# Long convolution with an FFT beside a gated MLP, forward and backward: transforms that share weights run jointly over 256 columns, spectra products are written in place, and the slots are ordered anew

## The chip, the cores and the metric

One core of a Trainium2 chip runs the whole program. The metric is the device time of one execution in microseconds (us), lower is better. Before the change it is 1892.35 us, the median of three runs (1892.13 to 1892.92).

The engines that matter are TensorE (PE; PEld stands for its weight loads), VectorE (DVE), ScalarE (ACT) and the DMA queue of SyncE (SP).

## The reference, cut to what matters

All tensors are bfloat16. S = 2048, D = 1024, F = 3584.

```
xn  = layernorm(x)
out = x + xn * (fftconv(kshift * v, ssm_k) + kshift * v * ssm_D) + W_down(relu(xn W_gate) * (xn W_up))
kshift[t] = sum over 4 taps of k[t - i] * shift_k[i]
```

The kernel returns `out` and the gradients of x, k, v, shift_k, ssm_k, ssm_D, W_gate, W_up and W_down for a given `grad_out`. The convolution is causal and is done per channel with a transform of length 4096 over the zero-padded sequence. Three spectra are needed in each channel: H of the filter, K of kv = kshift * v, and G of g = grad_out * xn. Three products are transformed back:

- Y = H * K gives y, which scales xn in the output;
- GKV = conj(H) * G gives the gradient of kv, and from it those of k, v and the taps;
- GH = conj(K) * G gives the gradient of the filter.

## The kernel before, in words

Class `LnMlp` does the layer norm and the MLP: `hidden` (gate, up and the gradient of h, with loops over 14 half blocks), then `grad_down` and `grad_in` (weight gradients), then `out_phase` and `grad_x`. Its matmuls are 128 x 128 weights by 512 columns. They are cut into steps of eight matmuls; after each step the generator yields 1730 (ns).

Class `ABranch` does the convolution in eight groups of 128 channels. Each transform of length 4096 is two matmul stages with a rearrangement between them:

- `fwd1` and `fwd1_filter`: stage one with the weights `R`, in 32 x 64 tiles of the array, 8 matmuls of 512 columns a slot. ScalarE (`act`, L76) takes the result from PSUM to a tile `B`.
- `flip`: VectorE transposes blocks of 32 x 32 (L298), in two halves.
- `fwd2`: stage two with the weights `FW`, in 64 x 32 tiles, 64 matmuls of 128 columns a slot. H, G and K have each two slots.
- `turn` and `cmul`: VectorE prepares and multiplies two spectra (all through the helper `tt`, L80). `cmul` works in two halves; a half is five pieces: two wide products t, twice a product u with its sum, and last a pair of sums that write the result.
- `inv_a`: first stage back, with the weights `IA` in 32 x 64 tiles, again 64 matmuls of 128 columns in each of two slots. ScalarE takes it to a tile `C`, and `flip` follows.
- `inv_b` (weights `RB`) and `inv_b_chan`: last stage back, to time order and to channel order.

`halo`, `tap_sums`, `tap_diagonals` and `taps` make the shifted k and the tap gradients.

`slots` is the order of one group, written out by hand: a list of pairs (TensorE work, VectorE work). The main loop takes MLP steps and counts down a budget; when it is used up it inserts the next slot. A slot costs 1900 of the budget in `hidden`, so that most slots are one step apart and some are two. In the dense phase, `grad_down` and `grad_in`, a slot with TensorE work costs 1760 and one without 1250, so that two slots can follow each other with no step between. Inside this stretch each engine runs its instructions in program order.

The convolution's PSUM pool has two tiles of two banks (`ps`, tag aps), and the MLP four of one bank. Five tiles of a pool `frm` hold spectra and, earlier, the rows of x for the layer norm; three of a pool `big` hold B, C and the flipped data in turn.

MLP work on VectorE in `hidden`: after an up step L972 and L974 (the gate's mask and the product h), after a gradient step L1067 (which follows the evacuation L1066 on ScalarE), after a gate step none. In the dense phase there is none.

Of the kernel before, what the change touches and what calls it, by code (L numbers as in the profile page):

```python
# [48 lines left out]
class ABranch:  # L49
# [48 lines left out]
    def open(self):  # L98
        R = "right"
        self.con = self.pool("a_con", 1, side=R)  # L100
        self.lng = self.pool("a_lng", 1, side=R)
        self.ld = self.pool("a_ld", 1, side=R)
        self.ts = self.pool("a_ts", 3, side=R)
        self.big = self.pool("a_big", 3, side=R)
        self.frm = self.pool("a_frm", 5, side=R)
        self.tmp = self.pool("a_tmp", 2, side=R)
        self.xp = self.pool("a_xt", 1, side=R)
        self.sm = self.pool("a_sm", 2, side=R)
        self.ps = self.pool("a_ps", 2, space=bass.MemoryType.PSUM)

# [180 lines left out]
    def flip(self, st, key, src):  # L291

        dst = st[key] = self.big.tile([P, NB1, P], BF16, name="flp", tag="big")
        df = dst[:].rearrange("p k c -> p (k c)").bitcast(F32).rearrange("p (k cp) -> p cp k", cp=64)
        sf = src.rearrange("p cp r i -> p (cp r i)").bitcast(F32).rearrange("p (cp r) -> p cp r", cp=64)
        for c0 in range(0, 64, 32):
            self.pri.late()
            self.pri.pin(self.nc.vector.transpose(out=df[:, c0:c0 + 32, :], in_=sf[:, c0:c0 + 32, :]))  # L298
            yield
# [36 lines left out]
    def fwd2(self, st, key, flp):  # L336
        F, Bf = self.form(key), st[flp]
        st[key] = F
# [14 lines left out]
    def form(self, name):  # L353
        return self.frm.tile([P, 8, 2, 2, P], BF16, name=name, tag="frm")

    def turn(self, st, name, b, sign):

        F, plus, minus = st[name], ALU.add, ALU.subtract
        for i in range(2):
            x = F[:, :, b, i]  # L360
            self.tt(x, x, F[:, :, 1 - b, 1 - i], plus if (i == 0) == (sign < 0) else minus)

    def cmul(self, st, m, n, conj, name):

        M, N = st[m], st[n]
        Q = st[name] = self.form(name)
        e, f = (1, 0) if conj else (0, 1)
        for hf in range(2):
            g = slice(4 * hf, 4 * hf + 4)
            M0 = M[:, g, 0:1].to_broadcast([P, 4, 2, 2, P])  # L370
            t = []
            for i in range(2):
                t.append(self.tmp.tile([P, 4, 2, 2, P], BF16, name="t%d" % i, tag="tmp"))
                self.tt(t[i][:], M0, N[:, g, :, ::-1] if i else N[:, g], ALU.mult)
                yield
            for i in range(2):
                u = self.sm.tile([P, 4, 2, P], BF16, name="u", bufs=1)
                self.tt(u[:], M[:, g, 1], N[:, g, e, ::-1] if i else N[:, g, e], ALU.mult)
                self.tt(t[i][:, :, f], t[i][:, :, f], u[:], ALU.add)
                yield  # L380
            for i in range(2):
                self.tt(Q[:, g, :, i], t[i][:, :, :, 0], t[i][:, :, :, 1], ALU.add if conj == (i == 0) else ALU.subtract)
            yield

    def inv_a(self, st, key, q_name):
        C = st[key] = self.big.tile([P, 64, 4, 8, 2], BF16, name="C", tag="big")
        Q = st[q_name]
# [17 lines left out]
    def inv_b(self, st, key, flp):  # L405
        dst, Cf = self.ttile(key), st[flp]
# [12 lines left out]
    def inv_b_chan(self, st, flp):  # L419
        dst, Cf = self.ttile("ghn"), st[flp]  # L420
        st["ghn"] = dst
        dv = dst[:, 0:16, :].rearrange("p r c -> p (r c)").rearrange("p (n1 n2) -> p n1 n2", n2=NB1)
        for n0 in range(0, NB1, 16):
# [4 lines left out]
            yield  # L428
# [48 lines left out]
    def steps(self):  # L477
# [19 lines left out]
        self.pri.strict = True  # L497
        self.begin(nx)
        for gi in range(self.NG):
            st, nx = nx, None  # L500
# [7 lines left out]
    def begin(self, st):  # L508
        st["ksh"] = self.lng.tile([P, 16, P], BF16, name="ksh")
        st["tk"] = self.taps(st, st["ksh"], st["kp"], [(3, 0), (2, 1), (1, 2), (0, 3)])  # L510
        st["f1h"] = self.fwd1_filter(st)

    MERGED = 3

    def slots(self, st, gi):
        last = gi + 1 == self.NG
        kp, gt = st["kp"], st["gt"]

        def next_filter():
            if not last:  # L520
                st["nx"] = self.load_filter(gi + 1)

        def next_g():
            if not last:
                self.load_g(st["nx"])

        def next_xn():
            if not last:
                self.load_xn(st["nx"])

        def next_v():
            if not last:
                self.load_v(st["nx"])

        def next_k():
            if not last:
                self.load_k(st["nx"])
                self.load_taps(st["nx"])

        def next_gate():  # L540
            if not last:
                self.gate_grad(st["nx"])

        def start_kvt():
            kvt = st["kvt"] = self.ttile("kvt")
            self.tt(kvt[:, 0:16, :], st["ksh"][:], st["vt"][:], ALU.mult)

        def start_gv():
            gv = self.ttile("gv")
            self.tt(gv[:, 0:16, :], st["gkv"][:, 0:16, :], st["ksh"][:], ALU.mult)  # L550
            st["gv"] = gv

        def start_gks():
            gks = st["gks"] = self.ttile("gks")
            self.tt(gks[:, 0:16, :], st["gkv"][:, 0:16, :], st["vt"][:], ALU.mult)

        def store_y():
            self.store_time(self.y_d, st["cg"], st["yt"])

        if gi and gi <= self.MERGED:  # L560
            self.begin(st)
        tk, f1h = st["tk"], st["f1h"]
        f1g = self.fwd1(st, "Bg", gt)
        if gi <= self.MERGED:
            yield f1h, None if gi else tk
            yield f1h, tk
            yield None, self.both(lambda: self.add_D(st), tk)
            yield None, tk
            yield None, tk
        flH = self.flip(st, "fH", st["Bh"][:].rearrange("p b x cp n i -> p (b x cp) n i"))  # L570
        f2H = self.fwd2(st, "H", "fH")
        if gi == 0:
            yield None, flH
            yield None, flH
            yield None, tk
            yield None, tk
            yield f2H, None
            yield None, next_filter
            yield f2H, lambda: self.gate_grad(st)
            yield f1g, None  # L580
            yield None, None
            yield f1g, None
            flG = self.flip(st, "fG", st["Bg"][:].rearrange("p b cp u r i -> p (b cp) (u r) i"))
            yield None, next_g
            yield None, flG
            yield None, flG
        else:
            yield f1g, flH
            yield None, self.both(next_filter, flH)
            yield f1g, tk  # L590
            yield next_g, tk
            yield f2H, tk if gi <= self.MERGED else None
            flG = self.flip(st, "fG", st["Bg"][:].rearrange("p b cp u r i -> p (b cp) (u r) i"))
            yield None, flG
            yield f2H, flG
        yield None, start_kvt
        f2G = self.fwd2(st, "G", "fG")
        yield f2G, None
        yield None, next_xn
        yield f2G, None  # L600
        f1k = self.fwd1(st, "Bk", st["kvt"])
        yield f1k, lambda: self.turn(st, "G", 0, -1)
        q = self.cmul(st, "H", "G", True, "GKV")
        yield None, q
        yield f1k, q
        yield None, q
        yield None, q
        flK = self.flip(st, "fK", st["Bk"][:].rearrange("p b cp u r i -> p (b cp) (u r) i"))
        yield None, flK
        yield None, flK  # L610
        yield None, q
        yield None, q
        f2K = self.fwd2(st, "K", "fK")
        yield f2K, q
        yield None, q
        yield f2K, q
        iaG = self.inv_a(st, "Cg", "GKV")
        yield iaG, q
        yield None, lambda: self.turn(st, "H", 1, 1)
        qy = self.cmul(st, "H", "K", False, "Y")  # L620
        yield next_gate, qy
        yield iaG, qy
        yield None, qy
        yield None, qy
        yield None, qy
        flg = self.flip(st, "fCg", st["Cg"][:].rearrange("p cp q m i -> p cp (q m) i"))
        yield None, flg
        yield None, flg
        iaY = self.inv_a(st, "Cy", "Y")
        yield iaY, qy  # L630
        yield None, qy
        yield self.inv_b(st, "gkv", "fCg"), qy
        yield None, qy
        yield None, start_gv
        yield None, qy
        self.store_time(self.out_gv, st["cg"], st["gv"])
        yield None, start_gks
        qh = self.cmul(st, "K", "G", True, "GH")
        yield iaY, qh
        yield None, self.both(next_v, qh)  # L640
        yield lambda: self.halo(st), qh
        yield None, qh
        yield lambda: self.tap_sums(st), qh
        yield None, lambda: self.tap_diagonals(st)
# [883 lines left out]
```

## Time and profile before

| | busy, us | share of the span |
|---|---|---|
| TensorE matmul | 1861.8 | 99% |
| TensorE weight load (overlaps) | 870.3 | 46% |
| VectorE | 1047.2 | 55% |
| ScalarE | 616.0 | 33% |

The profiled span is 1889.3 us. The first convolution slot starts at 112.8 us and the last at about 1171; `hidden` ends at about 653, and `out_phase` begins at about 1305. VectorE is busy 64.9% of the first 100 us, 70 to 85% of each 100 us from 100 to 1100, and little later. A convolution line of the profile is that of the helper which records it (L72 for every matmul, L76 for every evacuation, L80 for every elementwise operation), so groups are told apart by the names of their tiles. Matmuls of different tiles of the array overlap: the busy time of such a group is the union, and the mean of one says nothing of the rate.

### The profile page before, as it was taken

To read this page: it belongs to the slowest core of one execution; us is meant where nothing else is said; L and a number is where in the kernel's file an instruction comes from. 1 tells how busy PE (TensorE), PEld (TensorE's weight loads), DVE (VectorE), ACT (ScalarE), POOL (GpSimd) and SP (SyncE) were. 2 spreads that over 40 slices of the span, in tenths; PEclk is the share of its full clock that TensorE was granted. 3 is DMA by queue.
4 is the path that set the end of the run, shared out by engine and by line. 5 is a ranking of instruction groups with operands and counts; after the bars stand their busy time and mean duration, and the time that the engine had idled before them with its cause. 6 is when DMAs were issued, how large, how long until landed. Compare 5 with 4: busy or idle time off the path is not lost.

```text
span 1889.3 us, 36593 instructions
## 1 busy us (share of the span) xinstructions
PE 1861.8 (99%) x15526; PEld 870.3 (46%) x15768; DVE 1047.2 (55%) x1528; ACT 616.0 (33%) x858; POOL 14.9 (1%) x37
## 2 busy tenths in 40 slices
PE   9999999999999999999999999999999999999999
PEld 4444444444444444444444444444444544444444
DVE  6667978987987886867767585000222232222222
ACT  5655345436435445454354543111000000000000
POOL 1000000000000000000000000000000000000000
PEclk9999999999999999999999999999999999999999
DMA  9897679878578657475564535923999955545553
GB/s 254 247 224 186 156 191 200 202 184 183 143 184 199 196 165 179 118 176 183 145 159 118 157 94 161 323 96 101 251 245 241 245 125 123 123 122 123 123 122 73
DMA packets 694052, 323.19 MB, mean 171 GB/s; under 512 B 524408, under 2 KB 663424, under 8 KB 693888
## 3 DMA queue, kind: packets, MB, share of 16 engines
q1 hardware_dynamic: 683392, 299.99, 64.2%
q10 hardware_dynamic: 9216, 16.65, 3.1%
q0 software_dynamic: 1280, 4.20, 0.6%
q8 instruction: 123, 2.02, 0.4%
q14 instruction: 41, 0.34, 0.1%
HBM read 143.79 MB, written 95.44 MB: 127 GB/s over the span
## 4 chain that ended last, share of the span: by engine, by line
PE 97%; issue 1%; DVE 1%; DMA 0%; ACT 0%; DVEq 0%
PE ps_x L1385 20%; PE ps_w L1158 20%; PE ps_h L868 10%; PE ps_u L868 10%; PE ps_g L868 10%; PE ps_o L1316 10%; PE ps_d L1158 9%; PE ps L72 6%; PE ps_d L1171 1%; PE ps_w L1171 1%; PE ps_r L1346 0%; DMA ugs<-ug_d 0%; PE pst_x L900 0%; DMA ln_x<-in_A_q_dram 0%; ACT ln_j L796 0%
## 5 line engine op out<-in xcount | busy, mean ns | idle before, releaser
L1158 PE MATMUL ps_w<-ugs,xn_nat 128*128 128x512 bf16 x1670 | 375.4, 379 | 5.6 <-issue 3.8
L868 PEld LDWEIGHTS <-xnT 128*128 128x128 bf16 x1792 | 171.0, 98 | 206.5 <-issue 4.1
L1158 PEld LDWEIGHTS <-xn_nat 128*128 128x128 bf16 x1728 | 164.6, 98 | 198.1 <-issue 4.9
L868 PE MATMUL ps_u<-wu,xnT 128*128 128x512 bf16 x866 | 202.8, 379 | 2.3 <-issue 1.1
L868 PE MATMUL ps_h<-wdT,goT 128*128 128x512 bf16 x862 | 201.7, 379 | 3.3 <-issue 2.2
L1403 ACT ACTIVATE w<-xn,m 128x512 f32<-128x512 bf16 x32 | 24.3, 807 | 553.0 <-issue 317.2
L868 PE MATMUL ps_g<-wg,xnT 128*128 128x512 bf16 x868 | 200.8, 379 | 2.8 <-issue 1.0
L1385 PE MATMUL ps_x<-wuT,guT 128*128 128x512 bf16 x878 | 197.5, 379 | 1.0
L1385 PE MATMUL ps_x<-wgT,ggT 128*128 128x512 bf16 x878 | 197.3, 379 | 0.9
L1316 PE MATMUL ps_o<-wd,hT 128*128 128x512 bf16 (+1 forms) x879 | 186.7, 372 | 0.9
L1158 PE MATMUL ps_d<-g_nat,hs 128*128 128x512 bf16 x735 | 168.0, 379 | 3.8 <-issue 2.9
L1308 DVE TENSOR_TENSOR ya<-ya,xe 128x1024 bf16<-128x1024 bf16 x16 | 11.1, 693 | 253.4 <-DMA xe<-xn_d 253.4
L1385 PEld LDWEIGHTS <-guT 128*128 128x128 bf16 x896 | 87.7, 98 | 105.7
L1385 PEld LDWEIGHTS <-ggT 128*128 128x128 bf16 x896 | 87.7, 98 | 105.5
L1316 PEld LDWEIGHTS <-hT 128*128 128x128 bf16 x896 | 87.7, 98 | 99.9
L868 PEld LDWEIGHTS <-goT 128*128 128x128 bf16 x896 | 84.8, 98 | 102.5 <-issue 4.2
L1387 DVE CUSTOM_DVE_ANT_0 gx<-ps_x,gy 128x512 f32<-128x512 f32 x32 | 22.1, 691 | 186.7 <-PE ps_x L1385 184.6
L1066 ACT CAST gh<-ps_h 128x512 bf16<-128x512 f32 x112 | 65.5, 587 | 173.2 <-PE ps_h L868 160.7
L1262 ACT CAST wi<-ps_w 128x512 bf16<-128x512 f32 x108 | 63.7, 590 | 172.4 <-PE ps_w L1158 163.5
L972 DVE SCALAR_TENSOR_TENSOR ru<-ru,ps_u 128x512 bf16<-128x512 bf16 x112 | 76.4, 682 | 68.4 <-PE ps_u L868 33.4
L76 ACT CAST C<-ps 128x1024 bf16<-128x1024 f32 x96 | 92.5, 1015 | 64.8 <-PE ps L72 63.4
L1158 PEld LDWEIGHTS <-hs 128*128 128x128 bf16 x768 | 71.9, 98 | 86.7 <-issue 4.0
(163 smaller groups left out, 1701.0 us busy)
## 6 DMA issues: line engine op xcount, KB each, us to landing
ug_d<-ru SPq DMA_DIRECT2D x112, 256.0 KB
ugs<-ug_d SPq DMA_DIRECT2D x112, 256.0 KB
wg<-in_B_W_gate_dram SPq DMA_DIRECT2D x56, 256.0 KB
wu<-in_B_W_up_dram SPq DMA_DIRECT2D x56, 256.0 KB
h_d<-ht SPq DMA_DIRECT2D x112, 128.0 KB
hs<-h_d SPq DMA_DIRECT2D x56, 256.0 KB
out_dram<-wi SPq DMA_DIRECT2D x56, 256.0 KB
gt<-in_grad_out_dram SPq DMA_DIRECT2D x32, 256.0 KB
```

The lines of the kernel that those rows point to most:

```text
L72: self.pri.pin(self.nc.tensor.matmul(out, lhsT=lhsT, rhs=rhs, start=start, stop=stop))
L76: self.pri.pin(self.nc.scalar.copy(out=out, in_=in_))
L868: self.pri.pin(self.nc.tensor.matmul(ps[:], lhsT=xT[:, kt * P:(kt + 1) * P], rhs=w(kt), start=(kt == 0), stop=(kt == self.DT - 1)), always ...
L972: self.pri.pin(nc.vector.scalar_tensor_tensor(out=ru[s][:, 1, :], in0=ru[s][:, 0, :], scalar=0.0, in1=ps[:], op0=ALU.is_gt, op1=ALU.mult))
L1066: self.pri.pin(nc.scalar.copy(out=gh[:], in_=ps[:]))
L1158: self.pri.pin(self.nc.tensor.matmul(ps[:], lhsT=lhsT(st), rhs=rhs(st), start=(st == 0), stop=(st == self.ST - 1)))
L1171: self.pri.pin(self.nc.tensor.matmul(ps[i][:], lhsT=lhsT(i, st), rhs=rhs(i, st), start=(st == 0), stop=(st == self.ST - 1)))
L1262: self.pri.pin(nc.scalar.copy(out=wo[0][:, d, :], in_=ps[:]))
L1316: nc.tensor.matmul(ps, lhsT=hT[:, kt, :], rhs=self.wd[:, kt, oc], start=(kt == 0), stop=(kt == self.FT - 1))
L1385: nc.tensor.matmul(ps, lhsT=T[:, kt, :], rhs=W[:, kt, oc], start=(i == 0), stop=(i == n - 1))
L1387: V.tensor_tensor_reduce(out=gx[:, oc], in0=ps, in1=gy[:, oc], scale=1.0, scalar=0.0, op0=ALU.add, op1=ALU.add, accum_out=m[:, ob:ob + 1])
L1403: nc.scalar.activation(out=w[:, oc], in_=xn[:, oc], func=ACT.Identity, scale=m[:, 7:8], bias=m[:, 6:7])
```

## The change: what it does and what it is for

G and K are transformed by the same weights FW, and GH and Y by the same weights IA. The changed kernel keeps G and K interleaved in one tile, so that one matmul can take the columns of both: 256 instead of 128, with one weight load. `fwd2_pair` does this for G and K, `inv_a_pair` for GH and Y, each in four slots of 32 matmuls, where there were four of 64. `fwd2` stays for H and `inv_a` for GKV. In the pair functions each slot writes to both PSUM tiles at once; in `inv_a_pair` the evacuation splits into four of 512 elements for each slot.

The five spectrum tiles of `frm` become one tile, the arena: two halves for flipped data, two for G and K, one for H. GH is written over G and Y over K, half by half. The rows of the layer norm move to a pool of their own, which is given back before the arena takes its place.

Since K and G have to be ready together, stage one of a group's kv moves to the end of the group before. The order of the slots is written anew; `inv_b_chan` becomes one slot. In the new order flK (flip of K) is followed directly by the first slot of `fwd2_pair`, the last piece of the last product by the third slot of `inv_a_pair`, and `start_kvt` directly by `fwd1` of kvt. In the diff tk and tg are the taps' pieces, q a product's pieces, fl* the flips.

```diff
+    def fwd2_pair(self):
+        for j in range(4):
+            ps = [self.ps.tile([P, 2, 2, 2, 2, 64], F32, name="ps2", tag="aps") for _ in range(2)]
+            for m in range(2):
+                for ri in range(2):
+                    for q in range(4):
+                        for e in range(2):
+                            rows, l = slice(64 * e, 64 * e + 64), 8 * q + 2 * j + m
+                            self.mm(ps[e][32 * q:32 * q + 32, m, :, :, ri, :], self.FW[rows, l, ri, :],
+                                    self.flp[rows, :, l, :].rearrange("p k (b c) -> p b k c", b=2))
+            for e in range(2):
+                self.act(self.GK[:, 2 * j + e].rearrange("p b k i (m c) -> p (b k i) m c", m=2),
+                         ps[e][:].rearrange("p m b k i c -> p (b k i) m c"))
+            yield
...
+    def inv_a_pair(self, Cs):
...
+                            self.mm(ps[q // 2][64 * e:64 * e + 64, q % 2, m].rearrange("p k b c -> p b k c"),
+                                    self.IA[rows, x, ri].rearrange("p a n -> p (a n)"),
+                                    self.GK[rows, 2 * j + e, :, :, ri, 64 * m:64 * m + 64],
+                                    start=ri == 0, stop=ri == 1)
+            for h in range(2):
+                for k in range(2):
+                    self.act(Cs[k][:, :, 2 * h:2 * h + 2, 2 * j:2 * j + 2, :],
+                             ps[h][:, :, :, k].rearrange("p q m b (cp i) -> p (b cp) q m i", i=2))
+            yield
...
     def slots(self, st, gi):
...
+        f2 = self.fwd2_pair()
+        yield f2, None
+        yield None, none if last else lambda: self.load_g(nx)
+        yield f2, None
+        yield None, none if last else lambda: self.load_xn(nx)
+        yield f2, None
+        yield None, lambda: self.turn(G, 0, -1, slice(0, 4))
...
+        yield f2, q
...
+        yield None, flg
+        yield None, flg
+        yield None, q
+        ibg = self.inv_b(st, "gkv", 0)
+        yield ibg, q
...
+        ia = self.inv_a_pair((Ch, Cy))
...
+        yield ia, tg
+        yield None, tg
...
+        yield ia, tg
...
+        q = self.cmul(H, K, False, K, 1)
+        yield None, q
+        yield None, q
+        yield None, q
+        yield None, q
+        yield None, q
...
+            yield ia, tk
             yield None, tk
+            yield ia, tk
             yield None, tk
+            yield f2H, tk
+        fly = self.flip_C(Cy, 0)
+        yield None, fly
+        yield f2H, fly
+        flh = self.flip_C(Ch, 1)
+        yield None, flh
+        yield self.inv_b(st, "yt", 0), flh
+        yield None, tk
+        self.store_time(self.y_d, st["cg"], st["yt"])
+        yield self.inv_b_chan(st, 1), tk
...
+        yield None, lambda: self.start_kvt(nx)
+        f1k = self.fwd1(nx, "Bk", nx["kvt"])
+        flG = self.flip_B(nx, "Bg", 0)
+        yield f1k, flG
+        yield None, flG
+        yield f1k, lambda: self.store_gh(st)
+        yield None, None
+        flK = self.flip_B(nx, "Bk", 1)
         yield None, flK
         yield None, flK
```

## The prediction, made before the changed kernel ran

> **What bounds the kernel now.** I read the page's busy times and its chain first, then the groups by shape on TensorE, then the timelines of weight loads, VectorE and TensorE around single slots.
>
> ```profile
> span 1889.3 us, 36593 instructions
> ...
> PE 1861.8 (99%) x15526; PEld 870.3 (46%) x15768; DVE 1047.2 (55%) x1528; ACT 616.0 (33%) x858; POOL 14.9 (1%) x37
> ...
> PE 97%; issue 1%; DVE 1%; DMA 0%; ACT 0%; DVEq 0%
> ```
>
> TensorE is busy 99% of the span and is 97% of the chain, so the time is its work plus whatever it is made to wait. In the stretch that holds the convolution (113 to 1172 us) VectorE is the next engine:
>
> ```profile
> 300.00:400.00 100.00, 98.41 (x1116) 46.47 (x1116) 85.44 (x117) 47.10 (x64) 0.41 (x1) 1.00 0.90 204
> ```
>
> The columns after the length are PE, PEld, DVE, ACT busy. VectorE has 15% to spare here and 29% at 1000 to 1100 us, so it keeps pace only where a slot of TensorE comes late enough after the VectorE work that it needs.
>
> The convolution's matmuls (all of L72) come in slots between steps of eight MLP matmuls. The two shapes that the change touches, the second for GKV and GH as well:
>
> ```profile
> L72 PE MATMUL ps<-flp,FW 64*32 64x128 bf16 x3072 | 36.4, 221 | 0.0
> ...
> L72 PE MATMUL ps<-Y,IA 32*64 32x128 bf16 x1024 | 12.4, 224 | 0.0
> ```
>
> Tiles overlap, so what a slot costs is read from the weight loads:
>
> ```profile
> 131.74 3.33 PEld L868 LDWEIGHTS <-xnT 128*128 128x128 bf16 x16
> 135.50 0.60 PEld L72 LDWEIGHTS <-FW 64*32 64x32 bf16 x64 [0.42 <-issue]
> 136.18 1.41 PEld L868 LDWEIGHTS <-goT 128*128 128x128 bf16 x8
> 138.01 0.12 PEld L72 LDWEIGHTS <-R 32*64 32x64 bf16 x8 [0.42 <-DVE gt L80]
> 138.36 3.14 PEld L868 LDWEIGHTS <-goT 128*128 128x128 bf16 x16 [0.23 <-issue]
> ```
>
> An undisturbed MLP matmul takes 0.216 us (3.45 us for 16 in the chain). From the end of the first line (135.07) to that of the third (137.59) are 2.52 us with eight of them: the FW slot cost 0.79. The R slot after it: 141.50 - 137.59 - 16 x 0.216 = 0.46. Done for all 192 slots, the medians are FW 0.79 (48 slots), IA 0.80 (48), R 0.46 (48), RB 0.66 (16), tap sums 1.11 (8), 0.47 for 16 matmuls of inv_b_chan; together 128.8 us, with no slot over 0.4 above its median. TensorE is hardly ever kept waiting.
>
> **What the Trainium skill says.** "TensorEngine Tiling (Array Packing)", Tiling Modes: 64x32 and 32x64 tiling give eight independent tiles, and a change of tiling mode drains TensorE. "TensorE: Matmul & The Clock Gate", Back-to-back issue gap: N/2.4 + 2.5 ns warm, 215.8 ns for 512 columns; the trace has 216. With both, R (one round of eight tiles at 213 ns by columns; 8 matmuls of 512 columns) leaves 0.25 us fixed, RB (16 x 512, two rounds) 0.24, the tap sums (64 x 128, 16 rounds of four tiles at 53 ns) 0.26: the trace agrees, eight abreast and about 0.25 us per switch. "PSUM — Partial Sum Buffer", Specifications: eight banks of 512 fp32 per partition; the convolution's two tiles of two banks, beside the MLP's four, leave no spare; no run here shows the limit itself. "TensorE: Matmul & The Clock Gate", Step-by-step: only weight loads move forward, matmuls stay in program order; so one slot that waits for VectorE holds back all MLP matmuls behind it.
>
> **The change part by part.**
>
> *Wider matmuls.* fwd2 of G and K and inv_a of Y and GH: per group 4 + 4 slots of 64 matmuls over 128 columns become 4 + 4 of 32 over 256. That is 2048 matmuls and weight loads fewer, 64 slots repriced. FW's 0.79 - 0.25 = 0.54 for eight rounds is 67 ns a round, 14 above the 53 by columns. Four rounds at 107 ns give 0.68 with no excess, 0.73 with 14 ns each. I take 0.70: 32 x 0.09 + 32 x 0.10 = 6 us gained (4 to 7; nothing if all the excess stays, 0.79).
>
> *Costs at nothing.* The in-place products, the arena and the split turn keep VectorE's work (the split adds some 0.1 us a group, beside matmuls). inv_b_chan in one slot: 2 x 0.47. ScalarE gets 16 evacuations of 512 for 8 of 1024 per group in inv_a_pair: 16 x 0.59 - 8 x 1.02 = 1.3 us a group more on an engine that is half idle. Loads lead their use by at least 14 slots of 1.7 us, about 24; the first loads took some 12 (hn issued at 100.4, used at 112.8).
>
> *The new order.* It shortens the lead of some VectorE results over the slot that needs them from two or more slots to one. How close the old order is:
>
> ```profile
> 552.69 0.68 DVE L972 SCALAR_TENSOR_TENSOR ru<-ru,ps_u 128x512 bf16<-128x512 bf16 x1
> 553.40 0.42 DVE L974 TENSOR_TENSOR ht<-ru 128x512 bf16<-128x512 bf16 x1
> 553.75 1.28 DVE L80 TENSOR_TENSOR GH<-t 128x1024 bf16<-128x1024 bf16 x2
> ```
>
> ```profile
> 549.93 3.62 PE L868 MATMUL ps_u<-wu,xnT 128*128 128x512 bf16 x15
> 553.39 1.89 PE L868 MATMUL ps_h<-wdT,goT 128*128 128x512 bf16 x8
> 555.21 0.76 PE L72 MATMUL ps<-GH,IA 32*64 32x128 bf16 x64
> ```
>
> GH was put after the first of these two up steps, two steps (3.45 us) ahead of its slot, and was ready at 555.03, 0.18 before it: VectorE first had to finish the up step's work. After the change the third inv_a_pair slot stands one step (1.73) after its last product (the last q, then `yield ia, tk`), with steps u, u, product, h, slot in group 0. With the same backlog it comes 1.73 - 0.18 = 1.5 us late. I added the durations (up 0.68 + 0.39, gradient product 0.65, u and t 0.70 + 0.66, wide products 1.18, pair of sums 1.28, flip 1.86 each when back to back) down the order in which VectorE and TensorE will work in the changed kernel, MLP work included; down the old order the same sum gives no wait, least slack 0.15 at this very slot.
> - Third inv_a_pair slot, groups 0, 1, 2: 1.4 + 1.7 + 1.5 = 4.7 us. In the dense phase (after hidden) no MLP work stands on VectorE and it runs ahead: nothing.
> - First fwd2_pair slot, one step after the second half of flK. In the dense phase: second fwd1 slot at T; its flip can start at T + 2.56, as in
>
> ```profile
> 144.48 1.95 DVE L298 STREAM_TRANSPOSE flp<-B 128x1024 f32<-128x1024 f32 x1 [1.14 <-ACT B L76]
> ```
>
>   after the slot at 141.92. Two halves end at T + 6.3; TensorE arrives after 0.46 and three steps, T + 5.6: 0.5 to 0.7 late, four times, 2.4. In hidden five steps lie between, enough where they are h, h, g, g, but 1.4 late in group 2 (u, u, h, u, u). With 0.2 at the first: 4.0.
> - fwd1 of kvt, one slot after kvt: 0.4 + 0.4 + 0.8; first inv_b of group 2 behind flg: 1.7; smaller ones 0.3. Together 3.6.
> - PSUM: inv_a_pair fills both tiles, and four evacuations at 0.53 take 2.1 us. Where dense puts one step of 1.73 between two such slots (seven times) the next waits 0.4; fwd2_pair 0.2 (four times); slots of fwd1 as before, but one pair with two matmuls between, 1.4. Net of some 2 us of such waits in the old order, +3.9.
>
> Behind each waiting slot the MLP matmuls queue in order, and nothing gives the time back. Sum: 12.3 + 3.9 = 16 us lost, 6 gained: +10, **1902 us**.
>
> **The rivals.**
> 1. *The waits are hidden.* If VectorE is less behind than I add up, only the columns count: 1892.4 - 6 = 1886. For it: old slack at the tightest slots never ran out. Against: the product at 553.75 shows a lead of two steps nearly used up, and one step is taken away.
> 2. *They cancel.* Half of the waits and the full gain: 8 - 6 = +2, 1894. For it: a wait lets VectorE catch up, so later ones shrink (my sum has that in it already).
> 3. *The wide slots gain nothing* (0.79 stays): 1892.4 + 16 = 1908. For it: FW's unexplained 0.11 us. Should 256 columns go only four abreast, 64 x 0.31 more: 1928; against it R and RB, eight abreast at 512.
>
> **How the numbers follow.** Forecast 0.58 (1898 to 1906, from 0.68 to 0.73 a slot and 3 us on the waits), rival 1 0.16, rival 2 0.13, rival 3 0.13. Faster 0.16 is rival 1, same 0.13 rival 2, slower 0.71 the rest. The range, 1886 to 1910, leaves out the lower half of rival 1 and the upper part of rival 3.
>
> **What would show it.** Right: slots of 256 columns at about 0.70 us with 32 weight loads; before the third inv_a_pair slot of groups 0 to 2 the weight load waits over 1 us with VectorE (a spectra product into the arena) as releaser, and before the first fwd2_pair slot with a flip; VectorE busy no longer than now. Wrong: weight loads in these slots released by "issue" alone, or fixed 256-column slots near 0.8. What would make it wrong most likely is a backlog on VectorE smaller than the sum of durations, or a saving in the switch of tiling that I priced the same.

## The result, and the profile after

The changed kernel takes 1908.28 us (median of six runs, 1906.21 to 1910.69) against 1892.48 for the kernel before on the same chip: 15.8 us slower, ratio 1.0084 (95% interval 1.0071 to 1.0097). The forecast was 1902, in a range of 1886 to 1910. Direction and main mechanism held; the size was 6 us short.

The page of the changed kernel, its first lines and the chain:

```profile
span 1908.9 us, 32808 instructions
...
PE 1884.1 (99%) x13720; PEld 855.2 (45%) x13720; DVE 1051.5 (55%) x1544; ACT 619.3 (32%) x922; POOL 14.9 (1%) x37
...
PE 91%; DVE 5%; issue 1%; ACT 1%; DMA 1%; SPq 0%; DVEq 0%
```

VectorE is busy as before (1051.5 for 1047.2 us), yet its share of the chain went from 1% to 5%, and TensorE's from 97% to 91%. The work did not grow; the chain now passes through work that others do while TensorE stands. The groups by shape, and the waits of TensorE in the stretch with the convolution (sum, number, longest):

```profile
L72 PE MATMUL ps<-arena,IA 32*64 32x256 bf16 x1024 | 24.1, 275 | 6.6 <-DVE dg L80 3.1 <-DVE arena L80 2.9
L72 PE MATMUL ps<-arena,FW 64*32 64x256 bf16 x1024 | 21.3, 272 | 3.3 <-DVE arena L306 3.3
```

```profile
PE ps L72 <- DVE arena L306: 4.9, 8, 1.4
PE ps_u L905 <- DMA wu<-in_B_W_up_dram: 4.1, 2, 2.3
PE ps L72 <- DVE dg L80: 3.1, 3, 1.8
PE ps L72 <- DVE arena L80: 2.9, 6, 0.8
```

The first and the last line are the two waits that the prediction was about: a flip (L306) and a spectra product (L80) that reach their slots late. The two between are new: weights of the MLP that come late by DMA, and `dg`, a piece of the tap gradients. None of the four is among the waits of TensorE in the profile before.

What a slot costs is read from the weight loads as before. Two slots of `inv_a_pair` in the changed kernel, one step apart:

```profile
715.08 8.08 PEld L1195 LDWEIGHTS <-hs 128*128 128x128 bf16 x38
723.59 0.38 PEld L72 LDWEIGHTS <-IA 32*64 32x64 bf16 x32 [0.42 <-issue]
724.16 1.41 PEld L1195 LDWEIGHTS <-hs 128*128 128x128 bf16 x8 [0.20 <-issue]
725.99 0.12 PEld L72 LDWEIGHTS <-IA 32*64 32x64 bf16 x5 [0.42 <-issue]
726.38 0.36 PEld L72 LDWEIGHTS <-IA 32*64 32x64 bf16 x27 [0.27 <-issue]
726.93 3.13 PEld L1195 LDWEIGHTS <-hs 128*128 128x128 bf16 x16 [0.20 <-issue]
```

From 723.16 (end of the first line) to 725.57 (end of the third) are 2.41 us; less 8 x 0.216 that is 0.68, an undisturbed slot of 32 matmuls over 256 columns, where one of 64 over 128 cost 0.80. The next slot breaks off after five weight loads, and 730.06 - 725.57 - 16 x 0.216 = 1.03: 0.36 more. That is the wait for PSUM: ScalarE's four evacuations of the slot before end at 726.32, and the sixth weight load comes at 726.38. Done for all slots, each against the median of its shape:

| us | before | after |
|---|---|---|
| slots | 192 | 184 |
| undisturbed cost | 126.2 | 119.0 |
| waits above it | 2.7 | 29.3 |
| sum | 128.8 | 148.2 |

The sums differ by 19.4, the profiled spans by 1908.9 - 1889.3 = 19.6. So the whole loss lies in the slots and the steps behind them, and it is waiting: 7.2 us are gained on wide matmuls, 26.6 lost to waits. By cause the waits after are:

| waits after the change | us |
|---|---|
| third `inv_a_pair` slot, groups 0 to 2 (1.39, 1.25, 1.14) | 3.8 |
| first `fwd2_pair` slot (1.45 in group 2, four of 0.53 to 0.54) | 3.6 |
| kvt, first `inv_b` of group 2 (1.62), `inv_b_chan` | 3.5 |
| PSUM (seven of 0.36, four of 0.26, one of 1.58, five of 0.20 to 0.29) | 6.4 |
| first `inv_a_pair` slot, groups 0 to 2, for `dg` (3.79, 0.93, 0.93) | 5.7 |
| MLP weights, around 326 to 347 us | 8.0 |

They add up to 31.0, 1.7 more than the 29.3 of the table. Of this 0.8 is the last slot, which the table has too low in both kernels, since the long run of matmuls behind it comes a little faster than 0.216 each; the rest was not traced. The first four rows were predicted, the last two were not. How each arises:

*A predicted one.* VectorE and then TensorE of the changed kernel at the third slot of `inv_a_pair` in group 0:

```profile
271.90 0.42 DVE L1011 TENSOR_TENSOR ht<-ru 128x512 bf16<-128x512 bf16 x1
272.24 1.28 DVE L80 TENSOR_TENSOR arena<-t 128x1024 bf16<-128x1024 bf16 x2
```

```profile
272.98 0.32 PE L72 MATMUL ps<-arena,IA 32*64 32x256 bf16 x8 [0.83 <-DVE arena L80]
273.58 0.53 PE L72 MATMUL ps<-arena,IA 32*64 32x256 bf16 x24 [0.28 <-DVE arena L80]
```

The pair of sums that writes the product ends at 273.52, held up by the up step's work ahead of it; the slot starts its last 24 matmuls right after. It is the line at 553.75 of before, with one step less ahead of it.

*The first one not foreseen.* VectorE, then TensorE, at the first slot of `inv_a_pair` in group 0:

```profile
228.09 1.93 DVE L306 STREAM_TRANSPOSE arena<-B 128x1024 f32<-128x1024 f32 x1
...
230.92 1.91 DVE L306 STREAM_TRANSPOSE arena<-B 128x1024 f32<-128x1024 f32 x1
232.68 0.67 DVE L1104 TENSOR_TENSOR ru<-ru,gh 128x1024 bf16<-128x1024 bf16 x1
233.27 0.28 DVE L80 TENSOR_TENSOR dg<-ps,ident 128x128 f32<-128x128 f32 x1
```

```profile
231.47 0.30 PE L72 MATMUL ps<-arena,IA 32*64 32x256 bf16 x4
233.60 0.63 PE L72 MATMUL ps<-arena,IA 32*64 32x256 bf16 x28 [1.82 <-DVE dg L80]
234.16 3.20 PE L905 MATMUL ps_h<-wdT,goT 128*128 128x512 bf16 x8
```

`tap_sums` leaves its result in one of the two PSUM tiles. `tap_diagonals`, whose first operation (`dg`, 0.28 us) reads it, stands in the order behind the two halves of the filter's flip, 1.9 us each. A slot of `inv_a_pair` needs both tiles, and matmuls run in order: four matmuls go to the free one, the other 28 wait. Then the eight MLP matmuls that follow take 3.20 us, not the 1.73 of a step: they run at about half their rate (more in the last section).

*The second.* The DMA queue of SyncE, then TensorE, in group 1:

```profile
322.33 1.80 SPq L88 DMA_DIRECT2D gt<-in_grad_out_dram  x2
...
324.98 1.93 SPq L898 DMA_DIRECT2D wg<-in_B_W_gate_dram  x4
326.96 3.32 SPq L88 DMA_DIRECT2D xt<-xn_d  x2
...
335.52 1.99 SPq L898 DMA_DIRECT2D wu<-in_B_W_up_dram  x4
```

```profile
338.67 1.30 PE L905 MATMUL ps_u<-wu,xnT 128*128 128x512 bf16 x4 [2.35 <-DMA wu<-in_B_W_up_dram]
341.69 5.28 PE L905 MATMUL ps_u<-wu,xnT 128*128 128x512 bf16 x12 [1.72 <-DMA wu<-in_B_W_up_dram]
```

The loads of g (`gt`) and of xn (`xt`) stand ahead of the MLP's weights in the one queue. In the kernel before they were issued at 301.43 and 317.28 and `wu` at 324.63:

```profile
317.28 2.46 SPq L88 DMA_DIRECT2D xt<-xn_d  x2
...
324.63 2.56 SPq L861 DMA_DIRECT2D wu<-in_B_W_up_dram  x4
```

Now they come right behind the filter's loads (at 317.32), and `wu` starts at 335.52, 11 us later, and too late.

### The profile page after: what moved, and what is told of

Read it like the earlier page. It is cut to its first block, busy times and chain, and to the rows that moved or that the text cites. A ratio compares the mean times of both kernels' runs of the same rounds, so it can differ in the third digit from the quotient of the medians.

```text
span 1908.9 us, 32808 instructions
## 1 busy us (share of the span) xinstructions
PE 1884.1 (99%) x13720; PEld 855.2 (45%) x13720; DVE 1051.5 (55%) x1544; ACT 619.3 (32%) x922; POOL 14.9 (1%) x37
## 4 chain that ended last, share of the span: by engine, by line
PE 91%; DVE 5%; issue 1%; ACT 1%; DMA 1%; SPq 0%; DVEq 0%
PE ps_x L1422 20%; PE ps_w L1195 19%; PE ps_o L1353 10%; PE ps_g L905 9%; PE ps_u L905 9%; PE ps_h L905 8%; PE ps_d L1195 8%; PE ps L72 5%; PE ps_d L1208 1%; DVE arena L306 1%; DVE ru L1009 1%; ACT C L76 1%; PE ps_w L1208 0%; ACT B L76 0%; DVE ht L1011 0%
## 5 line engine op out<-in xcount | busy, mean ns | idle before, releaser
L1195 PE MATMUL ps_w<-ugs,xn_nat 128*128 128x512 bf16 x1728 | 382.4, 379 | 0.0
L905 PE MATMUL ps_u<-wu,xnT 128*128 128x512 bf16 x896 | 209.0, 383 | 4.2 <-DMA wu<-in_B_W_up_dram 4.1
L905 PE MATMUL ps_h<-wdT,goT 128*128 128x512 bf16 x896 | 207.6, 381 | 0.0
L1195 PE MATMUL ps_d<-g_nat,hs 128*128 128x512 bf16 x768 | 172.5, 379 | 0.0
L306 DVE STREAM_TRANSPOSE arena<-C 128x1024 f32<-128x1024 f32 x48 | 89.8, 1939 | 87.6 <-ACT C L76 78.3
L76 ACT CAST C<-ps 128x512 bf16<-128x512 f32 (+1 forms) x160 | 96.5, 682 | 81.1 <-PE ps L72 75.3
```

Source lines behind the costliest of these rows:

```text
L76: self.pri.pin(self.nc.scalar.copy(out=out, in_=in_))
L905: self.pri.pin(self.nc.tensor.matmul(ps[:], lhsT=xT[:, kt * P:(kt + 1) * P], rhs=w(kt), start=(kt == 0), stop=(kt == self.DT - 1)), always ...
L1195: self.pri.pin(self.nc.tensor.matmul(ps[:], lhsT=lhsT(st), rhs=rhs(st), start=(st == 0), stop=(st == self.ST - 1)))
```

## The experiments

Each kernel is timed against the kernel before on the same chip. In the first set (the four experiments that follow the repeat) before took 1891.07 us, in the second (the repeat, all three edits together, and the next two) 1892.03, in the third (the last two) 1892.89. The 95% intervals reach 1.7 to 2.7 us to either side, so a difference of 3 or 4 us between two versions is near the limit of what the times alone can show. "Less" or "more than the changed kernel" is measured from its +15.8, except where its repeat is named.

**Repeat of the changed kernel** (no edit), beside the second set:

> The changed kernel as it is, once more, so that the others of this call have it on the same chip: 1906 to 1909.

1907.06 us, ratio 1.0081 (1.0067 to 1.0095): +15.0 us.

**The tap diagonals moved ahead of the flip.**

```diff
         yield lambda: self.tap_sums(st), q
+        yield None, lambda: self.tap_diagonals(st)
         if not last:
...
             yield None, flH
-        yield None, lambda: self.tap_diagonals(st)
```

> tap_diagonals stands directly after tap_sums, ahead of the two flips of H, instead of behind them. In the changed kernel's trace the first inv_a_pair slot of groups 0, 1 and 2 waits 3.8, 0.9 and 0.9 us for dg (VectorE) to free its PSUM tile, the first with TensorE at half clock for eight matmuls after it. My theory (TensorE is held up by VectorE results and PSUM tiles that come too late, and only these waits make the loss): about 5 us less than the changed kernel, 1903. Rival (VectorE is simply short of time in hidden, so a wait taken away here comes back at the next slot): within 1.5 us of the changed kernel, 1907 to 1908.

1902.83 us, ratio 1.0062 (1.0049 to 1.0074): +11.8, 4.0 less than the changed kernel. The interval touches that of the changed kernel, so the profile has to carry the argument. In it `dg` runs ahead of both flips and the first slot does not wait; the waits sum to 20.7:

```profile
227.19 0.28 DVE L80 TENSOR_TENSOR dg<-ps,ident 128x128 f32<-128x128 f32 x1
```

```profile
231.02 0.64 PE L72 MATMUL ps<-arena,IA 32*64 32x256 bf16 x32
```

The cause of this wait is shown: same work, same slots, another place for a 0.28 us reader of PSUM. The wait did not come back at another slot: the first rows of the table (third `inv_a_pair` slot, first `fwd2_pair` slot) are as long as before the edit.

**An empty slot more between VectorE work and the slot that needs it**, before the third slot of `inv_a_pair`, before `fwd1` of kvt and before the first slot of `fwd2_pair`, where the prediction puts the waits.

```diff
         yield None, q
+        yield None, None
         if last:
             yield ia, None
...
         yield None, lambda: self.start_kvt(nx)
+        yield None, None
         f1k = self.fwd1(nx, "Bk", nx["kvt"])
...
         yield None, flK
         yield None, flK
+        yield None, None
```

> One empty slot more at three places of each group: between flK and the first fwd2_pair slot, between the last product and the third inv_a_pair slot, between start_kvt and fwd1 of kvt. My theory: the waits there (3.6, 3.8 and 1.2 us in the trace) vanish, some 8 us less, 1900. Rival (waits only move to other slots): over 1906. A rival in which the loss is in the wide matmuls themselves: no change, 1908.

1895.44 us, ratio 1.0022 (1.0013 to 1.0031): +4.4, 11.4 less than the changed kernel, where 8 was expected. In the profile the waits of the third `inv_a_pair` slot, of kvt and all but one of those of the first `fwd2_pair` slot (0.54 left) are gone, 8 us. The shifted order also ended the PSUM wait of 1.58, four of the seven of 0.36, and halved the 1.62 of `inv_b`. Weights (7.98) and `dg` (2.12 and 1.04) remain. Here is the third slot of `inv_a_pair`, in one piece:

```profile
272.09 0.64 PE L72 MATMUL ps<-arena,IA 32*64 32x256 bf16 x32
```

So the short leads are the largest part of the loss, and an empty slot does not cost its 1.73 us: the MLP step that fills it has to be done anyway.

**The loads of g and xn some 20 slots later.**

```diff
-        yield None, none if last else lambda: self.load_g(nx)
+        yield None, None
         yield f2, None
-        yield None, none if last else lambda: self.load_xn(nx)
+        yield None, None
...
         yield None, flg
         yield None, flg
+        if not last:
+            self.load_g(nx)
         yield None, q
+        if not last:
+            self.load_xn(nx)
```

> The loads of g and xn for the next group are issued some 20 slots later (after flip of Cg). In the changed kernel's trace they stand in the SyncE queue beside the filter load and ahead of a weight load, and TensorE waits once 4.5 us for wg and wu near 334 to 342 us, and then runs some 11 matmuls at half clock, 7.4 us in all. If the place of these loads is the cause: 5 to 7 us less, 1902. If the weights are late for another reason (the transposing loads at the change of halves): no change, 1908.

1901.36 us, ratio 1.0054 (1.004 to 1.0067): +10.3, 5.5 less. `wg` and `wu` are issued 3 and 8 us earlier than in the changed kernel, and no matmul waits for them; `wu`:

```profile
327.44 3.13 SPq L902 DMA_DIRECT2D wu<-in_B_W_up_dram  x4
```

**Each matmul over 256 columns as two over 128, in the new order.**

```diff
-                            self.mm(ps[e][32 * q:32 * q + 32, m, :, :, ri, :], self.FW[rows, l, ri, :],
-                                    self.flp[rows, :, l, :].rearrange("p k (b c) -> p b k c", b=2))
+                            for k in range(2):
+                                self.mm(ps[e][32 * q:32 * q + 32, m, :, k, ri, :], self.FW[rows, l, ri, :],
+                                        self.flp[rows, k, l, :].rearrange("p (b c) -> p b c", b=2))
```

and in `inv_a_pair` the same, with the loop over k outside that over ri.

> The new order and the arena stay, but each matmul over 256 columns is done as two over 128 (2048 matmuls more, 64 slots of 64 again). My theory: the 64 slots cost 0.79 instead of 0.68 us, so 7 us more than the changed kernel, 1915, a little less where a longer slot shortens a wait. Rival (a slot's cost is its fixed part and columns, equal for both): 1908.

1917.66 us, ratio 1.014 (1.0126 to 1.0154): +26.6, 10.8 more than the changed kernel, where 7 was expected. Wide matmuls do gain, but this version is not the old slot in the new order. Its `inv_a_pair` slots cost 0.79 undisturbed, as before; its `fwd2_pair` slots cost 0.865, not 0.785. One of these slots, in the version with the three edits and narrow matmuls further down:

```profile
762.33 3.14 PEld L1204 LDWEIGHTS <-hs 128*128 128x128 bf16 x16
765.89 0.66 PEld L72 LDWEIGHTS <-FW 64*32 64x32 bf16 x64 [0.42 <-issue]
766.65 3.14 PEld L1204 LDWEIGHTS <-hs 128*128 128x128 bf16 x16
```

769.79 - 765.47 - 16 x 0.216 = 0.864. The edit in `fwd2_pair` has k as its innermost loop, so two matmuls in a row go to the same tile of the array; in the kernel before, and in the edited `inv_a_pair`, eight tiles take turns. That this order is what costs the 0.08 is likely, but no run tried the other one. For 32 slots it is 2.6 us, so the undisturbed slots of this version sum to 128.8 us, against 119.0 with wide matmuls: 9.8 of the 10.8.

**The first three edits together.**

> tap_diagonals early, an empty slot at the three places, and the loads of g and xn later, all together. My theory: only the column gain of 7 us and PSUM waits of the dense phase about as long as those of the kernel before are left, so 5 to 7 us less than the kernel before, 1885. Rival (VectorE's lateness comes back somewhere): 1890 or more.

1886.59 us, ratio 0.9972 (0.9961 to 0.9982): -5.4, faster than before. The three gains by themselves were 4.0 + 11.4 + 5.5 = 20.9; together they are 15.0 + 5.4 = 20.4. Within the noise they add, as three different waits would. The rival, 1890 or more, falls. The waits above undisturbed slots are down from 29.3 us to 5 or 6 in its profile.

**The same, and a wide slot in the dense phase priced at 2210**, so that it has one or two steps behind it.

```diff
-                yield self.DENSE[p is None] if self.dense else self.SLOT
+                yield (2210 if p is self.wide else self.DENSE[p is None]) if self.dense else self.SLOT
...
-        f2 = self.fwd2_pair()
+        f2 = self.wide = self.fwd2_pair()
...
-        ia = self.inv_a_pair((Ch, Cy))
+        ia = self.wide = self.inv_a_pair((Ch, Cy))
```

> As the one with all three, and in the dense phase a slot of fwd2_pair or inv_a_pair costs 2210 of the budget instead of 1760, so that two steps lie between two such slots. My theory: the PSUM waits of 0.36 and 0.26 us at these slots go away, 1 to 2 us less than with all three, 1883.5, unless the convolution's later end delays the load of W_down, which then shows as a wait before the first ps_o.

1884.47 us, ratio 0.9961 (0.9949 to 0.9974): -7.6. The interval overlaps that of the version without it. Its PSUM waits at wide slots are gone, but in its profile the up weights are late again in group 1 (5.0 us), and its five runs spread from 1882.98 to 1887.17. The slowest is the one in the profile, and the only one of the five whose mean granted clock was below 1.000 (0.999).

**The three edits with narrow matmuls.**

> As the one with all three, but with each matmul of 256 columns as two of 128. The price of the wide matmuls without the waits: my theory 7 us more than with all three (64 slots by 0.11), 1892; rival (a slot's cost is its fixed part and columns): the same as with all three.

1896.25 us, ratio 1.0022 (1.0013 to 1.0031), 9.7 more than with wide ones, where 7 was expected. The spans differ by 10.3. The undisturbed slots account for 9.8 of it (128.8 against 119.0): 7.2 for the width, and the 2.6 for the `fwd2_pair` slots of 0.865 described above.

**The best version, with the filter's load moved behind the third slot of `fwd2_pair`.** By the edit that is five slots later; the expectation says four.

```diff
-        nx = None if last else self.load_filter(gi + 1)
-        st["nx"] = nx
         f2 = self.wide = self.fwd2_pair()
...
         yield f2, None
         yield None, None
         yield f2, None
+        nx = None if last else self.load_filter(gi + 1)
+        st["nx"] = nx
```

> The best version so far (three lead changes, wide slots spaced apart), with the load of the next group's filter rows issued four slots later. In its profile these four loads took 8.05 us of the DMA queue just ahead of the loads of the up weights (issued at 327.69), and the up step behind them cost 5.0 us: 2.4 us of waits on the weights and the rest at half the matmul rate afterwards. Theory (the queue's order makes the weights late, and the half rate is the sequel of the wait): no matmul waits for weights, none runs at 0.43 us after it, about 1880 us. Rival 1 (the weights are late for another reason): 1884 to 1885. Rival 2 (only the wait is given back, the half rate has another cause): about 1882.

1882.44 us (1882.12 to 1882.66), ratio 0.9944 (0.9931 to 0.9956): -10.4, the fastest of all. `wu` is now issued at 319.17, and both the wait and the half rate behind it are gone; the 24 weight loads of the gate and up steps run through. The chain of its page, and the weight loads:

```profile
PE 98%; DVE 1%; DMA 0%; ACT 0%; issue 0%; DVEq 0%
```

```profile
327.99 4.86 PEld L912 LDWEIGHTS <-xnT 128*128 128x128 bf16 x24 [0.21 <-issue]
```

Waits in slots are 1.2 us, less than the 2.7 of the kernel before. The 7.2 of the wide matmuls and these 1.5 make 8.7, and the spans differ by 8.4. The median of 1882.44 is nearer to rival 2 than to the theory's 1880. But the version before this edit ran at half rate in one execution of five only, the profiled one, so its median had little half rate to give back; the profile is what tells the two apart, and it has neither wait nor half rate.

**The price of wide slots alone, on the changed kernel.** The budget edit above and nothing else.

> The changed kernel with nothing else altered than the budget of a slot of fwd2_pair or inv_a_pair in the dense phase, 2210 for 1760, so that at least one step and at times two follow it before the next. It prices the PSUM waits alone. Theory (a wide slot fills both PSUM tiles, and the next waits for their evacuation: seven times 0.36 and four times 0.26 us in the changed kernel's profile): 3.6 us less than the changed kernel's 1907 to 1908, about 1904. Rival (the wait only moves to another slot or is paid elsewhere): 1907 to 1908.

1903.38 us, ratio 1.0052 (1.0038 to 1.0065): +10.5, 4.5 to 5.3 less than the changed kernel. The PSUM waits at wide slots are gone in its profile, and with the shifted steps most of the one of 1.58 (0.42 left): together about 4.7 us. The rival falls; the wait does not move elsewhere. The weights and `dg` are as late as in the changed kernel.

## Why the prediction was right in direction and 6 us short

- **The main claim held.** The new order shortens leads, MLP matmuls queue behind each waiting slot, and nothing gives the time back. The empty slots alone took back 11.4 of the 15.8 us.
- **Wide slots: right, slightly under.** Forecast 0.70 (0.68 to 0.73); measured 0.674 for FW and 0.68 for IA, so 7.2 us, not 6. The unexplained 14 ns a round belong to the 128-column form: with the prediction's 0.25 fixed, (0.674 - 0.25) / 4 is 106 ns, the columns alone. The median 1908 equals the number of rival 3 (the wide slots gain nothing); it is not rival 3, as the slots of 0.674 and 0.68 show, and the narrow versions (10.8 and 9.7 us slower, of which 2.6 is the order of their loop). A total that fits does not choose between sums.
- **Third `inv_a_pair` slot: right in place and cause.** 1.4 + 1.7 + 1.5 forecast, 1.39 + 1.25 + 1.14 measured: 3.8 for 4.7 (4.6, as its three terms add up). VectorE was 0.4 less behind than forecast in the two later groups; why was not taken apart. In the dense phase nothing, as said.
- **First `fwd2_pair` slot: right.** 3.6 for 4.0; 1.45 for 1.4 in group 2, and 0.53 to 0.54 four times for 0.5 to 0.7.
- **kvt, `inv_b` and smaller: right in sum.** 3.5 for 3.6: `inv_b` 1.62 for 1.7 and kvt 0.13, 0.14, 0.88 for 0.4, 0.4, 0.8.
- **PSUM: right.** Net 3.7 for 3.9, with 0.36 for 0.4, 0.26 for 0.2 and 1.58 for 1.4.
- **What failed: two costs set at nothing.** "Loads lead their use by at least 14 slots": true of these loads, which were never late. But the question was what they stand in front of. They went ahead of the MLP's weights in the same queue, and those were late (8.0 us in the profile; 5.5 in the timed comparison). And the PSUM step counted evacuations by ScalarE alone, 0.53 us each; the tile of `tap_sums` is emptied by VectorE, behind two flips (5.7 us in the profile; 4.0 timed). Some 4.5 us of these two costs in the profile is no wait at all, but matmuls at half the clock behind the waits (9.0 busy us, last section), for which the prediction had no term.

Added up from the profile: -7.2 + 3.8 + 3.6 + 3.5 + 3.7 + 5.7 + 8.0 = 21.1, less the 1.7 that the rows have too much, 19.4 of the 19.6. Of what the prediction named it would have been +7.4, against the forecast's +10; the two missed costs bring the rest. The timed 15.8 is lower than the profiled 19.6 since the profiled execution of the changed kernel was the slowest of its six (1910.69 for a median of 1908.28), at a mean clock of 0.997 where the others had 0.998 or 0.999, and that of the kernel before (1891.05) was faster than its median.

## What to carry to other kernels

When an order written by hand moves a result to one step ahead of its use, add up what stands in front of it on its own engine, not its duration alone; such sums came out within 0.5 us a wait here, and filling the gap with work that had to be done anyway cost nothing. Ask of each moved transfer and each buffer not only whether it is in time itself, but who is queued behind it and who empties it. A faster inner step (7.2 us) is worth having only once the order around it is paid for: the same matmuls were 0.8% slower in one order and 0.6% faster in another.

## What the runs showed of the hardware

A short wait can cost twice. After the wait of 1.82 us for `dg` the next eight MLP matmuls took 3.20 us; after the waits for `wu` of 2.35 and 1.72 us weight loads came every 0.43 us, eleven in a row, twice the usual 0.216. The clock that the trace records was 0.50 from 234.61 to 238.02 us and from 340.42 to 347.25, and 1.00 otherwise once it had started up. The changed kernel around the first of these, with the busy time of PE, PEld, DVE, ACT and POOL, then the granted clock, the share of the DMA engines and GB/s:

```profile
231.19:234.61 3.42, 1.60 (x37) 0.69 (x36) 3.39 (x6) 0.99 (x2) 0.00 (x0) 1.00 0.89 253
234.61:238.02 3.41, 3.41 (x10) 1.21 (x9) 1.00 (x2) 2.23 (x5) 0.00 (x0) 0.50 1.16 305
```

The Trainium skill, "TensorE: Matmul & The Clock Gate", Part 1, tells of a clock at half rate after an idle window of some 3.4 us, watched in windows that run free of the program, and of 426.7 ns for 512 columns at that rate. The trace agrees on the rate (0.43 us) and on the windows: the changes of the clock lie whole multiples of 3.413 us apart (234.61 and 340.42 are 31 of them), and in each run this grid lies elsewhere against the program. But the page's advice of no gaps over about 3 us ("Why this matters for your kernels") is too wide here: 1.82 was enough, with busy matmuls on both sides.

It was not always enough. At this same slot the wait was 1.82 to 1.89 us in six profiles; three had half rate after it, three did not. The grid tells them apart. In the three with half rate the whole wait fell into one window, which had 1.82, 1.84 and 1.89 us idle. In the other three an edge of the grid split it, and no window had more than 1.69. Here is the version with empty slots, its grid counted back from the changes at 335.81 and 342.64:

```profile
230.00:233.41 3.41, 1.73 (x11) 0.60 (x9) 3.38 (x5) 0.98 (x2) 0.00 (x0) 1.00 1.06 239
233.41:236.82 3.41, 3.10 (x40) 1.64 (x42) 2.20 (x5) 2.54 (x5) 0.00 (x0) 1.00 0.99 307
```

Read so, the twelve profiles have, between their first and their last microseconds, nine changes to half rate. Each follows a window with 1.76 to 3.41 us idle, and no window with 1.73 or less is followed by one. So in these runs about half a window of idle time was enough, and how the grid happened to lie decided whether a wait of 1.8 us cost more than itself. The ends of matmuls are modelled, so the edge between 1.73 and 1.76 is no sharper than that, and no experiment moved a wait against the grid.
